# Loading four key units in other pieces, and keeping a row of x on the chip

## The chip, the cores and the metric

The kernel runs on one core of a Trainium2 chip. The metric is the device time of one execution in microseconds (us). Engines are named as in the profile: PE (TensorE), DVE (VectorE), ACT (ScalarE), POOL (GpSimd) and SP (SyncE). SP computes nothing here; it issues nearly all transfers from the chip's memory (HBM), and the core's 16 DMA engines carry them out.

## The reference

One token goes through two blocks, and their outputs are added to x. Block A is attention with cached keys and values: 16 query heads on 8 key/value heads, 65536 keys of 256 numbers a head. Block B is a gated feed-forward layer with a scalar gate r.

```
xn = layernorm(A_x)                                # 1 x 448
q  = xn @ wq                                       # 16 heads of 256
scores = q . k_cache * 256**-0.5                   # two query heads to a key head
o  = softmax(scores) . v_cache
attn = o @ wo                                      # 4096 -> 448
r  = xn @ w_r
ffn = xn + (silu(xn @ w_gate) * (xn @ w_up)) @ w_down * sigmoid(r)
out = x + attn + ffn
```

K and V are 268 MB each in bf16; everything else together is 12 MB. x is used twice: normalized at the start, and in the last sum.

## The kernel before

**Tiling.** Each of the 8 heads' 65536 keys is cut into 4 units. A unit is 128 keys on each of 128 partitions, 64 KB a partition and 8 MB in all. There are 32 units of K (K0 to K31) and 32 of V. They pass through a ring of three slots of one unit each: the even K units use slot 0, the odd ones slot 1, and the V units slot 2. At the start slot 2 also holds wq and small rows such as x; at the end slots 0 and 1 serve for V as well, and slot 2 for the weights of the last stretch.

**Turns.** The program has 32 turns, one for each K unit. In turn u the unit K_u is scored: 8 sets of 16 columns each, and a half of the unit is 4 sets. For each set PE transposes the keys (written `k_T`, 16 transposes), DVE and ACT copy the result out of PSUM to `kt_all`, and PE multiplies by the queries (`k_QK`). From turn 4 on, after the first four sets, there is a V block: PE weighs the unit V_(u-4) with the softmax numerators of its head (`pe_V`, two runs of 32 matmuls into `ps_o`). So the first four turns have no V work; the scores of head 0 are complete in turn 4, whose first sets still contain the last product of K3, its maximum (`m1p`, `gmax`, `negmax`) and the exponentials (ACT, L590). Only then can the V block of turn 4 run.

**What sets the order.** The order on each engine is written out by hand: the functions append waits (`W`) and operations (`O`) to one list for each engine, and `emit` turns the lists into loops. In PE's loop the even and the odd turns have code of their own for the sets, and share the V block. SP's list is a plain sequence: `item` appends the waits a load needs, then the load, and SP stands still at a wait until it is met, with all later loads behind it. The sequence is wq, K0, K1, K2, K3, V0, K4, K5, V1, K6, V2, K7 and so on. The waits are:

- K_u needs its slot: `FREE` of u-2 says that PE has transposed all 8 sets of K_(u-2), `FREEH` that it has transposed the first 4.
- V_t needs `VFREE` of t-1: PE has finished the V block of V_(t-1). V0 needs the end of the setup, since wq lies in its slot.
- PE in turn u waits for the landing of K_u, in the V block for the landing of V_(u-4). Each wait is on a semaphore that the load raises when it lands.

**Pieces.** `HALVED` lists the K units that are loaded in two halves by two transfers with semaphores of their own (`slot0` or `slot1`, and `half0` or `half1`). PE waits for the first half before set 0 and for the second before set 4 (L774). Of a halved unit the first half's load waits for `FREEH` only. Before the change the units 0 to 4 are halved, and all others come whole.

**Setup and end.** In the setup DVE normalizes x (`dve_setup`), PE turns it into a column (`XNT`), multiplies by wq (`QROW`) and puts q where the turns need it (`QT`). `middle` is the part of the end that handles the feed-forward layer; there x is wanted again, normalized (`XN_AGAIN`, L881) and as it is (`YX`, L890). For that the row x is loaded a second time into slot 2, behind w_down and on its semaphore `wd`. PE adds the resulting sum into `ps_s` (`FIN_BASE`) before it turns to the last two V units. PSUM has eight banks; `ps_m` and `ps_s` are two of them and hold small results of each turn in columns below 288.

Of the kernel before, what the change touches and what calls it, by code (L numbers as in the profile page):

```python
# [7 lines left out]
ALU = mybir.AluOpType  # L8
# [4 lines left out]
CH = 64  # L13
# [11 lines left out]
def bass_parallel_sum__gqa_block_cached__moe_arch_mod__decode_kernel(  # L25
# [41 lines left out]
    NT = U * (Hkv - 1)  # L67
    NU = U * Hkv
    NTB = NG
    UH = U + 1  # L70
    HALVED = (0, 1, 2, 3, 4)
    assert rep == 2 and NH == 2 and U * SBN == NPP and U % 2 == 0
    assert 2 * D % P == 0 and RP % 2 == 1 and FK % 2 == 0 and Hq % 2 == 0 and FB <= 512
    inv_sqrt_dh = float(Dh) ** -0.5
# [8 lines left out]
    FO = rep * NH  # L83
    WOA = (Hkv - 1) * WON
    WEN = WOA + WGN + 2 * WDN
    assert WEN + 2 * D <= SLOT
    DC = D // 4

    sb = []
# [11 lines left out]
    wo_all = slots[2][:, 0:WOA]  # L101
    wg_area = slots[2][:, WOA:WOA + WGN]
    wd_area = slots[2][:, WOA + WGN:WOA + WGN + 2 * WDN]
    x_again = slots[2][0:1, WEN:WEN + D]
    xn_again = slots[2][0:1, WEN + D:WEN + 2 * D]
    wo_end = kt_all[:, 0:WON]
    temp = [WQN]

# [84 lines left out]
    ps_m = PS_("ps_m", [P, 512], FP32)  # L193
    C_XNT, C_BC, C_TOT, C_OT, C_Q, C_BIG = 0, 16, 18, 22, 28, 64
    C_HT = C_Q
    assert C_Q + NH * Hq + 4 <= C_BIG and C_HT + FK <= C_BIG and C_BIG + P <= 512

    sems = {}
# [5 lines left out]
        sems[name] = s.__enter__()  # L204
        return name

    for n_ in ["pe", "act", "dve", "pool", "qk", "jt", "evq", "exp", "pc", "qc", "sc", "w0", "out", "wq", "wg", "wo", "wd", "we0", "we1", "we2", "wo2", "wo3", "half0", "half1", "res"]:
        SEM(n_)
    for i in range(NTB):
        SEM(f"ev{i}")  # L210
# [85 lines left out]
    def k_item(u):  # L296
        need = [("FREE", u - 2)] if u >= 2 else ()
        if u >= 2 and u in HALVED:
            need = {0: [("FREEH", u - 2)], 1: need}
        slot_item("k", u, u % 2, [("slot%d" % (u % 2), CH), ("half%d" % (u % 2), CH)] if u in HALVED else None, need)  # L300

    def v_item(t):
        slot_item("v", t, 2, None, [("VFREE", t - 1)] if t else [("QT",), ("R",), ("CONST",)])

    WQ1 = WQN // 4
    item("wq", [(wq_area[:, a:b], flat_src(A_wq, WQN)[:, a:b], "wq") for a, b in ((0, WQ1), (WQ1, WQN))])
    for u in range(U):
        k_item(u)
    v_item(0)
# [61 lines left out]
    def dve_setup():  # L371
        v = nc.vector
        W("dve", "z_m1p")
        O("dve", "XEZ", lambda it: v.memset(xe_row[:, :, :, :], 0.0), "sc")
        O("dve", "PSQ_ZERO", lambda it: v.memset(ps_q[:, :], 0.0), "ev0")
        O("dve", "PSO_ZERO", lambda it: v.memset(ps_o[:, :], 0.0), "ev1")
        O("dve", "s2z0", lambda it: v.memset(s2[0][:, :], 0.0), "ev2")
        O("dve", "pssz", lambda it: v.memset(ps_s[:, :], 0.0))
        O("dve", "S2Z", lambda it: v.memset(s2[1][:, :], 0.0))
        W("dve", "DMA", "w0")  # L380
        O("dve", "xf", lambda it: v.tensor_copy(out=x_f, in_=x_row))
        W("dve", "xf")
        O("dve", "mean", lambda it: v.tensor_reduce(out=stat[0:1, 0:1], in_=x_f, axis=AX.X, op=ALU.add))
        W("dve", "mean")
        O("dve", "negmean", lambda it: v.tensor_scalar(out=stat[0:1, 7:8], in0=stat[0:1, 0:1], scalar1=-1.0 / D, scalar2=None,
                                                       op0=ALU.mult))
        W("dve", "negmean")
        O("dve", "xc", lambda it: v.tensor_scalar(out=xc_f, in0=x_f, scalar1=stat[0:1, 7:8], scalar2=None, op0=ALU.add))
        W("dve", "xc")
        O("dve", "sumsq", lambda it: v.tensor_tensor_reduce(out=xn_f, in0=xc_f, in1=xc_f, scale=1.0, scalar=0.0,  # L390
                                                            op0=ALU.mult, op1=ALU.add, accum_out=stat[0:1, 1:2]))
        W("dve", "sumsq")
        O("dve", "VPE", lambda it: v.tensor_scalar(out=stat[0:1, 2:3], in0=stat[0:1, 1:2], scalar1=1.0 / D, scalar2=EPS,
                                                   op0=ALU.mult, op1=ALU.add))
# [13 lines left out]
        alias("dve", "XE")
        O("dve", "R", lambda it: v.tensor_tensor_reduce(out=x_f, in0=xn_bf, in1=wr_row, scale=1.0, scalar=0.0,
                                                        op0=ALU.mult, op1=ALU.add, accum_out=stat[0:1, 5:6]))  # L410
# [32 lines left out]
    def pe_setup():  # L443
        W("pe", "XE")
        W("pe", "CONST")

        def xnt(it):
            for c in range(2 * NE):
                ins = mm(ps_m[0:P, C_XNT + c:C_XNT + c + 1],
                         lhsT=xe_row[0:1, :, :, :].rearrange("o b c p -> o (b c) p")[:, c, :],  # L450
                         rhs=sel_bf[0:1, 0, 0:1], start=True, stop=True)
            return ins

        O("pe", "XNT", xnt, n=16 * U)
        W("pe", "XNTSB")
        W_item("pe", "wq")

        def qrow(it):
            for h in range(RP):
                for j in range(NG):  # L460
                    ins = mm(q_rows[32 * j:32 * j + rep, :], lhsT=xnT_sb[:, 2 * h:2 * h + 2], rhs=wq_area[:, (NG * h + j) * QN:(NG * h + j + 1) * QN],
                             start=h == 0, stop=h == RP - 1, tile_position=(0, 32 * j))
            return ins

        W("pe", "PSQ_ZERO")
        O("pe", "QROW", qrow, "jt", 2)
        W("pe", "QROWSB")

        def qt(it):
            half = Hq * NH // 2  # L470
            for f in range(half // NG):
                w = q_row[0:QROWS, f // NH * Dh:(f // NH + 1) * Dh].rearrange("s (x f) -> s x f", f=NH)[:, :, f % NH]
                ins = mm(ps_m[0:P, C_Q:C_Q + 2 * half].rearrange("p (i j f) -> p j i f", i=rep, j=NG)[:, :, :, f], lhsT=w,
                         rhs=sel_bf[0:QROWS, :, :], start=True, stop=True)
            return ins

        O("pe", "QT", qt, "qk", 2)
        W("pe", "PSO_ZERO")
        W("pe", "S2Z")
        W("pe", "KZ")  # L480
        W("pe", "z_q")
# [191 lines left out]
    def pe_attn():  # L673
# [9 lines left out]
        oT_i = oT_b.rearrange("p f h i -> p f (h i)")  # L683
        at = [C_BIG + sum(NH * h * h for _, h, _ in WPIECES[:k]) for k in range(len(WPIECES) + 1)]
        sums = picked[:, at[-1] - C_BIG:at[-1] - C_BIG + FO * (Hkv - 1)]
        assert at[-1] <= 512 and at[-1] - C_BIG + FO * (Hkv - 1) <= 256

        def regroup(it):
            for k, (_, h, h0) in enumerate(WPIECES):
# [80 lines left out]
    def k_sets(u, sets, at):  # L770
        ap = slots[u % 2]
        for q in sets:
            if q % CSETS == 0:
                W_item("pe", ("k", u, 0) if q == 0 else ("k", min(u, UH - 1 - (UH - 1 - u) % 2), 1))  # L774
            s = u * SETS + q
            for n, m in enumerate(TORD):
                k_T(s, m, ap, q * SETN)
                if n == NG - 1 and (q + 1) % CSETS == 0:
                    alias("pe", "FREE" if q == SETS - 1 else "FREEH", u, sem=f"t{m}")
                if (q, n) in at:  # L780
                    at[(q, n)]()
                if n == 1:
                    k_QK(s - 1)
            k_JT(s - 2)
# [89 lines left out]
    def middle(T):  # L874
# [2 lines left out]
        pe_ffn1()  # L877
        pe_ffn_hT()
        pe_ffn2()
        W_item("dve", "wd")  # L880
        O("dve", "XN_AGAIN", lambda it: nc.vector.tensor_scalar(out=xn_again, in0=x_again, scalar1=stat[0:1, 7:8], scalar2=stat[0:1, 4:5],  # L881
                                                                op0=ALU.add, op1=ALU.mult))
        W("dve", "XN_AGAIN")
        W("dve", "FFN2")
        W("dve", "ATTN")
        W("dve", "SIG")
        O("dve", "YS", lambda it: nc.vector.scalar_tensor_tensor(
            out=sum_f, in0=ps_y, scalar=stat[0:1, 6:7], in1=xn_again, op0=ALU.mult, op1=ALU.add))
        W("dve", "YS")
        O("dve", "YX", lambda it: nc.vector.tensor_tensor(out=sum_f, in0=sum_f, in1=x_again, op=ALU.add))  # L890
        W("dve", "YX")
        O("dve", "SUM", lambda it: nc.vector.tensor_tensor(out=sum_f, in0=ps_a, in1=sum_f, op=ALU.add))
        W("pe", "SUM")
        W("pe", "SCOPY", T)
# [324 lines left out]
```

## Time and profile before

| | |
|---|---|
| Median of 3 runs | 1275.97 us (1275.46 to 1275.99) |
| Profiled execution | 1275.56 us, span 1274.2 us |
| PE, DVE, ACT busy | 74%, 45%, 26% |
| Transfers | 549.03 MB, queue busy 99.7%, 431 GB/s |
| Granted PE clock, mean | 0.887 of full speed |

The span is the time from the first to the last instruction in the trace of one profiled execution; the 1.36 us by which that execution is longer lie outside of it. Busy shares are means over the whole span; PE's is not an amount of useful work, since its matmuls overlap. The transfers' line counts the time in which packets were on the way, as a share of the span of the 16 DMA engines.

### The profile page before, as it was taken

The page shows a single profiled execution, that of the slowest core. Times are in us where ns is not written, and L with a number is a line of the kernel's source. Part 1 is how long each engine was busy: PE and PEld are TensorE (multiplying, and loading weights), DVE is VectorE, ACT ScalarE, POOL GpSimd, SP SyncE. Part 2 cuts the span into 40 slices and gives each one's busy share as a digit, 9 for nine tenths or more (in the row PEclk, how much of TensorE's full clock was granted, in tenths as well). Part 3 has the DMA queues.
Part 4 walks back from the last instruction along what each step waited for, and adds up shares of the span by engine and source line. Part 5 has one row for each costly group of instructions (what it writes and reads, how often), then busy time and mean ns, then how long its engine had stood idle before and what let it go on. Part 6 is the DMA issues. An engine that isn't in the chain of part 4 may idle for free.

```text
span 1274.2 us, 21262 instructions
## 1 busy us (share of the span) xinstructions
PE 939.5 (74%) x8812; PEld 577.8 (45%) x8812; DVE 571.6 (45%) x1086; ACT 329.3 (26%) x432; POOL 9.1 (1%) x38
## 2 busy tenths in 40 slices
PE   4997977678777679777778776687676687766744
PEld 2665544445444445444445444454344454444412
DVE  5775644355344454443454444454444543434410
ACT  1333422132222322222222222222222222222200
POOL 2000000000000000000000000000000000000000
PEclk9998988789888898888898888898888988888885
DMA  9999999999999999999999999999999999999998
GB/s 405 429 435 426 451 430 430 432 432 434 442 430 430 432 432 436 440 430 430 432 432 440 436 432 428 432 432 440 436 432 428 434 430 446 432 430 428 431 437 364
DMA packets 11812, 549.18 MB, mean 431 GB/s; under 512 B 1303, under 2 KB 1690, under 8 KB 2202
## 3 DMA queue, kind: packets, MB, share of 16 engines
q1 hardware_dynamic: 11796, 549.03, 99.7%
q8 instruction: 7, 0.11, 0.0%
q14 instruction: 3, 0.02, 0.0%
q10 hardware_dynamic: 6, 0.00, 0.0%
HBM read 549.03 MB, written 0.00 MB: 431 GB/s over the span
## 4 chain that ended last, share of the span: by engine, by line
DMA 78%; PE 20%; issue 1%; DVE 0%; ACT 0%; SPq 0%; DVEq 0%
DMA ring<-in_A_v_cache_dram 74%; PE ps_o L441 13%; DMA ring<-in_A_k_cache_dram 5%; PE ps_t L441 5%; PE ps_q L441 1%; PE ps_m L441 1%; PE ps_s L441 0%; DVE kt_all L504 0%; ACT S_sb L590 0%; SPq L983 0%; DVE m1p L560 0%; DVE S_sb L558 0%; ACT p_sb L600 0%; DVE kt_all L932 0%; DVE diag L575 0%
## 5 line engine op out<-in xcount | busy, mean ns | idle before, releaser
L441 PE MATMUL ps_t<-ident_f,ring 128*128 128x128 f32 x4096 | 583.8, 288 | 76.8 <-DMA ring<-in_A_k_cache_dram 76.4
L504 DVE COPY kt_all<-ps_t 128x1024 bf16<-128x1024 bf16 x768 | 489.8, 684 | 293.2 <-PE ps_q L441 287.5
L441 PEld LDWEIGHTS ps_t<-ident_f,ring 128*128 128x128 f32 x4096 | 454.2, 144 | 251.5 <-issue 133.8
L506 ACT ACTIVATE kt_all<-ps_t 128x1024 bf16<-128x1024 bf16 x256 | 261.9, 1023 | 490.1 <-PE ps_t L441 489.8
L441 PE MATMUL ps_o<-ring,p_sb 128*4 128x512 bf16 x2048 | 183.1, 522 | 217.8 <-DMA ring<-in_A_v_cache_dram 214.7
L441 PEld LDWEIGHTS ps_o<-ring,p_sb 128*4 128x4 bf16 x2048 | 54.7, 103 | 313.5 <-issue 292.3
L441 PE MATMUL ps_q<-kt_all,q_pad 128*16 128x512 bf16 x2056 | 168.0, 402 | 4.7 <-DVE kt_all L504 1.3
L613 DVE RECIPROCAL rs<-ps_m 128x4 f32<-128x4 f32 x29 | 5.3, 183 | 277.3 <-PE ps_m L441 277.3
L600 ACT ACTIVATE p_sb<-S_sb 128x128 bf16<-128x128 bf16 x64 | 18.9, 307 | 274.7 <-PE ps_o L441 274.4
L648 DVE CAST ob_sb<-ps_o 100x512 bf16<-100x512 f32 x29 | 20.1, 692 | 101.3 <-PE ps_o L441 101.3
L441 PEld LDWEIGHTS ps_q<-kt_all,q_pad 128*16 128x16 bf16 x2056 | 28.8, 86 | 51.7 <-issue 26.7
L532 ACT ACTIVATE s<-ps_q 112x512 bf16<-112x512 f32 x33 | 19.7, 597 | 118.3 <-PE ps_q L441 118.3
L441 PEld LDWEIGHTS ps_m<-rowsum,ones_f 128*128 128x128 f32 x58 | 12.3, 264 | 23.1 <-issue 23.1
L590 ACT ACTIVATE S_sb<-S_sb,negmax 128x512 bf16<-128x512 bf16 x16 | 13.3, 856 | 23.3 <-DVE negmax L584 23.3
L441 PE MATMUL ps_m<-diag,ones_f 2*128 2x2 f32 x58 | 11.1, 258 | 11.2 <-DVE diag L575 11.2
L441 PEld LDWEIGHTS ps_m<-diag,ones_f 2*128 2x128 f32 x58 | 8.6, 184 | 18.1 <-DVE diag L575 18.1
L560 DVE TENSOR_REDUCE m1p<-S_sb (+1 forms) x33 | 13.9, 422 | 4.4
L441 PE MATMUL ps_m<-rowsum,ones_f 128*128 128x4 f32 x58 | 14.9, 326 | 0.0
L558 DVE CAST S_sb<-ps_s 128x256 f32 (+1 forms) x33 | 13.7, 414 | 1.9 <-PE ps_s L441 1.9
L441 PE MATMUL ps_m<-sel_bf,ring 1*128 1x1 bf16 (+1 forms) x12 | 0.6, 168 | 13.6 <-DVE ring L406 12.8
L441 PE MATMUL ps_s<-sel_bf,s 128*128 128x64 bf16 x132 | 9.2, 193 | 0.7 <-ACT s L532 0.7
L532 ACT ACT_TABLE_LOAD x7 | 9.0, 1283 | 1.3 <-issue 1.2
(97 smaller groups left out, 132.4 us busy)
## 6 DMA issues: line engine op xcount, KB each, us to landing
ring<-in_A_k_cache_dram SPq DMA_DIRECT2D x10, 4096.0 KB, 28.6
ring<-in_A_v_cache_dram SPq DMA_DIRECT2D x2, 4096.0 KB, 27.9
ring<-in_A_wq_dram SPq DMA_DIRECT2D x1, 2688.0 KB, 11.1
ring<-in_B_w_gate_dram SPq DMA_DIRECT2D x1, 1568.0 KB, 16.4
ring<-in_B_w_up_dram SPq DMA_DIRECT2D x1, 1568.0 KB, 19.8
ring<-in_B_w_down_dram SPq DMA_DIRECT2D x1, 1568.0 KB
ring<-in_A_wo_dram SPq DMA_DIRECT2D x1, 1344.0 KB, 35.2
ring<-in_A_wo_dram SPq DMA_DIRECT2D x1, 1120.0 KB, 24.9
```

Source lines behind the costliest of these rows:

```text
L441: return pe.matmul(*a, **k)
L504: O(e, ("EV", s, m), lambda it: nc.vector.tensor_copy(out=kt[:, :], in_=tb[:, :]), f"ev{m}")
L506: O(e, ("EV", s, m), lambda it: nc.scalar.activation(out=kt[:, :], in_=tb[:, :], func=ACTF.Copy), f"ev{m}")
L532: O("act", ("EVQ", u), lambda it: nc.scalar.activation(out=s2[u % 2][0:SROWS, :], in_=ps_q[0:SROWS, :], func=ACTF.Copy), "evq")
L558: O("dve", ("SCOPY", u), lambda it: nc.vector.tensor_copy(out=S_sb[:, at(it, SBN), :], in_=ps_sn), "sc")
L560: O("dve", ("SMAX", u), lambda it: nc.vector.tensor_reduce(out=m1p[:, :, at(it, 1)], in_=S_sb[:, at(it, SBN), :].rearrange("p n i -> p i n ...
L590: O("act", ("EXP", h, i), lambda it, i=i: nc.scalar.activation(out=S_sb[:, :, i], in_=S_sb[:, :, i], func=ACTF.Exp, bias=negmax[:, i:i + 1 ...
L600: O("act", ("PC", t, c), lambda it: nc.scalar.activation(out=p_sb[:, c, :, :], in_=S_sb[:, n:n + CH, :], func=ACTF.Copy), "pc")
L613: O("dve", ("RS", t), lambda it: nc.vector.reciprocal(out=rs[:, :, :], in_=ps_m[0:P, C_TOT:C_TOT + NH * rep]))
L648: O("dve", ("OB", t), lambda it: nc.vector.tensor_copy(out=ob_sb[0:OROWS, :], in_=ps_o[0:OROWS, :]))
```

## The change

Three things are changed.

1. `HALVED` holds only unit 3. The units 1, 2 and 4 are loaded whole, on one semaphore each. Unit 0 comes in three parts of 32, 32 and 64 columns (`FIRST`) on the semaphores `slot0`, `part` and `half0`. PE waits for them before sets 0, 2 and 4. Since even turns share their code, each even turn has these two further waits with constant values, which unit 0's landing has met for good.
2. The two loads of wq have semaphores of their own, `half1` and `wq`. The first stands in for the second half of unit 1 (`items[("k", 1, 1)]`), so that the values for which the odd turns wait in front of set 4 keep their steps.
3. x is not loaded again. In the setup DVE copies the row in two halves of 224 numbers, as fp32, to the last columns of `ps_m` and `ps_s` (`XKEEP`), and at the end `XN_AGAIN` and `YX` read it there, in two pieces each.

```diff
-    HALVED = (0, 1, 2, 3, 4)
+    HALVED = (3,)
+    FIRST = (CH // 2, CH // 2, CH)
...
+    C_X = 512 - D // 2
+    X_HALVES = [(ps_m[0:1, C_X:512], 0, D // 2), (ps_s[0:1, C_X:512], D // 2, D)]
...
-        slot_item("k", u, u % 2, [("slot%d" % (u % 2), CH), ("half%d" % (u % 2), CH)] if u in HALVED else None, need)
+        parts = [("slot%d" % (u % 2), CH), ("half%d" % (u % 2), CH)] if u in HALVED else None
+        slot_item("k", u, u % 2, parts if u else list(zip(("slot0", "part", "half0"), FIRST)), need)
...
-    item("wq", [(wq_area[:, a:b], flat_src(A_wq, WQN)[:, a:b], "wq") for a, b in ((0, WQ1), (WQ1, WQN))])
+    for k, (a, b, sem) in enumerate(((0, WQ1, "half1"), (WQ1, WQN, "wq"))):
+        item(("wq", k), [(wq_area[:, a:b], flat_src(A_wq, WQN)[:, a:b], sem)])
+    items[("k", 1, 1)] = items[("wq", 0)]
...
-    item("wd", [(wd_area.rearrange("p (s x) -> p s x", s=2), B_w_down.rearrange("(s p t) n -> p s (t n)", s=2, p=P), "wd"), (x_again, A_x[0], "wd")])
+    item("wd", [(wd_area.rearrange("p (s x) -> p s x", s=2), B_w_down.rearrange("(s p t) n -> p s (t n)", s=2, p=P), "wd")])
...
+        W("dve", "pssz")
+        for k, (kept, a, b) in enumerate(X_HALVES):
+            O("dve", ("XKEEP", k), lambda it, kept=kept, a=a, b=b: v.tensor_copy(out=kept, in_=x_row[:, a:b]))
         W("dve", "SQRT")
...
-            if q % CSETS == 0:
-                W_item("pe", ("k", u, 0) if q == 0 else ("k", min(u, UH - 1 - (UH - 1 - u) % 2), 1))
+            if q == 0:
+                W_item("pe", ("k", u, 0))
+            elif u % 2 == 0 and q * SETN in (FIRST[0], FIRST[0] + FIRST[1]):
+                W_item("pe", ("k", 0, 1 if q * SETN == FIRST[0] else 2))
+            elif u % 2 and q == CSETS:
+                W_item("pe", ("k", min(u, HALVED[-1]), 1))
...
-        W_item("dve", "wd")
-        O("dve", "XN_AGAIN", lambda it: nc.vector.tensor_scalar(out=xn_again, in0=x_again, scalar1=stat[0:1, 7:8], scalar2=stat[0:1, 4:5],
+        for k, (kept, a, b) in enumerate(X_HALVES):
+            W("dve", "XKEEP", k)
+            O("dve", ("XN_AGAIN", k), lambda it, kept=kept, a=a, b=b: nc.vector.tensor_scalar(
+                out=xn_again[:, a:b], in0=kept, scalar1=stat[0:1, 7:8], scalar2=stat[0:1, 4:5], op0=ALU.add, op1=ALU.mult))
```

SP's first loads before the change, with the semaphores that stand ahead of them (128x16384 is a half of a unit, 128x32768 a whole one; `sem_t2` carries `FREE` and `FREEH`, `sem_pe` carries `VFREE`):

```order
L983 DMA ring<-in_A_wq_dram 128x3584
L983 DMA ring<-in_A_wq_dram 128x10752
L983 DMA ring<-in_A_k_cache_dram 128x16384 x4
L983 DMA ring<-in_A_k_cache_dram 128x16384 [waits sem_t2] x4
L983 DMA ring<-in_A_v_cache_dram 128x32768 [waits sem_pool,sem_dve,sem_qk]
L983 DMA ring<-in_A_k_cache_dram 128x16384 [waits sem_t2] x2
L983 DMA ring<-in_A_k_cache_dram 128x32768 [waits sem_t2]
L983 DMA ring<-in_A_v_cache_dram 128x32768 [waits sem_pe]
```

The same place after it:

```order
L1001 DMA ring<-in_A_wq_dram 128x3584
L1001 DMA ring<-in_A_wq_dram 128x10752
L1001 DMA ring<-in_A_k_cache_dram 128x8192 x2
L1001 DMA ring<-in_A_k_cache_dram 128x16384
L1001 DMA ring<-in_A_k_cache_dram 128x32768
L1001 DMA ring<-in_A_k_cache_dram 128x32768 [waits sem_t2]
L1001 DMA ring<-in_A_k_cache_dram 128x16384 [waits sem_t2] x2
L1001 DMA ring<-in_A_v_cache_dram 128x32768 [waits sem_pool,sem_dve,sem_qk]
L1001 DMA ring<-in_A_k_cache_dram 128x32768 [waits sem_t2] x2
L1001 DMA ring<-in_A_v_cache_dram 128x32768 [waits sem_pe]
```

The order of the units is the same. Unit 0 is three loads, the units 1, 2 and 4 one each, and the load of V1 (the last row of both) still follows K5.

PE's code of the even turns around the V block, before the change (`ps_o` is the V block, the `ps_t` row behind it is the first transpose of set 4):

```order
L441 MATMUL ps_o<-ring,p_sb 4x512 [waits sem_slot2,sem_dve,sem_pc]
L441 MATMUL ps_o<-ring,p_sb 4x512 x31
L441 MATMUL ps_m<-rowsum,ones_f 128x4 [waits sem_pc,sem_dve]
L441 MATMUL ps_o<-ring,p_sb 4x512 [waits sem_slot2,sem_pc]
L441 MATMUL ps_o<-ring,p_sb 4x512 x31
L1108 UNCONDITIONAL_BRANCH
L1142 COMPARE_AND_BRANCH
L1086 REGISTER_ALU
L441 MATMUL ps_t<-ident_f,ring 128x128 [waits sem_ev0,sem_half0]
```

And after it:

```order
L449 MATMUL ps_o<-ring,p_sb 4x512 [waits sem_slot2,sem_dve,sem_pc]
L449 MATMUL ps_o<-ring,p_sb 4x512 x31
L449 MATMUL ps_m<-rowsum,ones_f 128x4 [waits sem_pc,sem_dve]
L449 MATMUL ps_o<-ring,p_sb 4x512 [waits sem_slot2,sem_pc]
L449 MATMUL ps_o<-ring,p_sb 4x512 x31
L1126 UNCONDITIONAL_BRANCH
L1160 COMPARE_AND_BRANCH
L449 MATMUL ps_t<-ident_f,ring 128x128 [waits sem_ev0,sem_half0]
```

The V block stands where it stood, behind four sets of its turn. The wait for `half0` in front of set 4 is now for a constant, so the register operation ahead of it is gone.

DVE's last steps on x at the end, before the change:

```order
L761 CAST hT_sb<-ps_m 128x7x2 [waits sem_pe]
L881 TENSOR_SCALAR ring<-ring,stat 1x448 [waits sem_wd]
L887 SCALAR_TENSOR_TENSOR ring<-ps_t,stat,ring 1x448 [waits sem_ev3,sem_pe,sem_dve]
L890 TENSOR_TENSOR ring<-ring 1x448 [waits sem_dve]
L892 TENSOR_TENSOR ring<-ps_q,ring 1x448 [waits sem_dve]
```

And after it:

```order
L770 CAST hT_sb<-ps_m 128x7x2 [waits sem_pe]
L895 TENSOR_SCALAR ring<-ps_m,stat 1x224
L895 TENSOR_SCALAR ring<-ps_s,stat 1x224
L902 SCALAR_TENSOR_TENSOR ring<-ps_t,stat,ring 1x448 [waits sem_pe,sem_ev3,sem_dve]
L906 TENSOR_TENSOR ring<-ring,ps_m 1x224 [waits sem_dve]
L906 TENSOR_TENSOR ring<-ring,ps_s 1x224
L910 TENSOR_TENSOR ring<-ps_q,ring 1x448 [waits sem_dve]
```

Two of the five steps are cut in two, and the wait for `wd` is gone from DVE.

## Rows read from the trace of the kernel before

**Rows 1.** The page: span, transfer queue, bytes, chain by engine.

```profile
span 1274.2 us, 21262 instructions
...
q1 hardware_dynamic: 11796, 549.03, 99.7%
...
HBM read 549.03 MB, written 0.00 MB: 431 GB/s over the span
...
DMA 78%; PE 20%; issue 1%; DVE 0%; ACT 0%; SPq 0%; DVEq 0%
```

**Rows 2.** Chain of waits, 79 to 250: start us, us, what.

```profile
79.63 40.50 DMA ring<-in_A_k_cache_dram
...
140.15 28.39 DMA ring<-in_A_v_cache_dram
...
174.92 32.32 DMA ring<-in_A_v_cache_dram
...
213.15 32.79 DMA ring<-in_A_v_cache_dram
```

**Rows 3.** Single issues on L983 (K2's first half, V0, K5): start, landing.

```profile
L983 SPq DMA_DIRECT2D ring<-in_A_k_cache_dram x1: 328/328/328, 35.0 to 35.0; - x1
...
DMA to landing us min/median/max: 26.9/26.9/26.9
...
L983 SPq DMA_DIRECT2D ring<-in_A_v_cache_dram x1: 349/349/349, 68.9 to 68.9; - x1
...
DMA to landing us min/median/max: 41.5/41.5/41.5
...
L983 SPq DMA_DIRECT2D ring<-in_A_k_cache_dram x1: 327/327/327, 112.3 to 112.3; - x1
...
DMA to landing us min/median/max: 36.9/36.9/36.9
```

**Rows 4.** Timeline, turns 0 to 2: start us, us, what [idle before <-releaser].

```profile
11.76 0.38 DVE L400 CAST ring<-ring 1x448 bf16<-1x448 f32 x1
...
22.08 1.97 PE L441 MATMUL ps_t<-ident_f,ring 128*128 128x128 f32 x8 [4.13 <-DMA ring<-in_A_k_cache_dram]
...
46.35 0.33 SPq L983 DMA_DIRECT2D ring<-in_A_k_cache_dram  x1
...
68.46 0.33 SPq L983 DMA_DIRECT2D ring<-in_A_k_cache_dram  x1
```

**Rows 5.** Timeline of turn 4, up to V0's last matmuls.

```profile
120.17 1.97 PE L441 MATMUL ps_t<-ident_f,ring 128*128 128x128 f32 x8 [7.89 <-DMA ring<-in_A_k_cache_dram]
...
133.78 0.15 DVE L584 TENSOR_SCALAR negmax<-ps_m 128x2 f32<-128x2 f32 x1
...
136.06 1.90 PE L441 MATMUL ps_o<-ring,p_sb 128*4 128x512 bf16 x32 [1.99 <-ACT p_sb L600]
...
138.21 1.90 PE L441 MATMUL ps_o<-ring,p_sb 128*4 128x512 bf16 x32
```

**Rows 6.** Timeline of turn 5: its first transposes and negmax.

```profile
149.69 2.25 PE L441 MATMUL ps_t<-ident_f,ring 128*128 128x128 f32 x16
...
162.44 0.15 DVE L584 TENSOR_SCALAR negmax<-ps_m 128x2 f32<-128x2 f32 x1
```

**Rows 7.** First load's issue, size and landing; windows (PEclk, DMA share, GB/s last).

```profile
0.81 0.39 SPq L983 DMA_DIRECT2D ring<-in_A_wq_dram  x1
...
ring<-in_A_wq_dram SPq DMA_DIRECT2D x1, 896.0 KB, 5.1
...
0.80:1.80 1.00, 0.00 (x0) 0.00 (x0) 0.21 (x1) 0.20 (x1) 0.91 (x7) 1.00 0.03 1
...
115.00:125.00 10.00, 4.83 (x25) 3.65 (x26) 1.29 (x2) 1.89 (x4) 0.00 (x0) 0.51 0.99 424
```

**Rows 8.** Timeline of the end: the sum with x, and PE's wait behind it.

```profile
1221.90 0.61 DVE L890 TENSOR_TENSOR ring<-ring 1x448 f32<-1x448 f32 x1
...
1227.62 5.48 PE L441 MATMUL ps_o<-ring,p_sb 128*4 128x512 bf16 x64 [4.05 <-DMA ring<-in_A_v_cache_dram]
```

More of the change, by code (lines that the diff above doesn't have):

```diff
@@ L69, in bass_parallel_sum__gqa_block_cached__moe_arch_mod__decode_kernel @@
     NTB = NG
-    UH = U + 1
-    HALVED = (0, 1, 2, 3, 4)
+    HALVED = (3,)
+    FIRST = (CH // 2, CH // 2, CH)
     assert rep == 2 and NH == 2 and U * SBN == NPP and U % 2 == 0
@@ L85, in bass_parallel_sum__gqa_block_cached__moe_arch_mod__decode_kernel @@
     WEN = WOA + WGN + 2 * WDN
-    assert WEN + 2 * D <= SLOT
+    assert WEN + D <= SLOT
     DC = D // 4
@@ L103, in bass_parallel_sum__gqa_block_cached__moe_arch_mod__decode_kernel @@
     wd_area = slots[2][:, WOA + WGN:WOA + WGN + 2 * WDN]
-    x_again = slots[2][0:1, WEN:WEN + D]
-    xn_again = slots[2][0:1, WEN + D:WEN + 2 * D]
+    xn_again = slots[2][0:1, WEN:WEN + D]
     wo_end = kt_all[:, 0:WON]
@@ L195, in bass_parallel_sum__gqa_block_cached__moe_arch_mod__decode_kernel @@
     C_HT = C_Q
+    C_X = 512 - D // 2
+    X_HALVES = [(ps_m[0:1, C_X:512], 0, D // 2), (ps_s[0:1, C_X:512], D // 2, D)]
+    assert C_BIG + P <= C_X and SBN * rep <= C_X
     assert C_Q + NH * Hq + 4 <= C_BIG and C_HT + FK <= C_BIG and C_BIG + P <= 512
@@ L205, in SEM @@
         return name
-    for n_ in ["pe", "act", "dve", "pool", "qk", "jt", "evq", "exp", "pc", "qc", "sc", "w0", "out", "wq", "wg", "wo", "wd", "we0", "we1", "we2", "wo2", "wo3", "half0", "half1", "res"]:
+    for n_ in ["pe", "act", "dve", "pool", "qk", "jt", "evq", "exp", "pc", "qc", "sc", "w0", "out", "wq", "wg", "wo", "wd", "we0", "we1", "we2", "wo2", "wo3", "half0", "half1", "part", "res"]:
         SEM(n_)
@@ L455, in pe_setup @@
         W("pe", "XNTSB")
-        W_item("pe", "wq")
+        W_item("pe", ("wq", 0))
+        W_item("pe", ("wq", 1))
         def qrow(it):
@@ L685, in pe_attn @@
         sums = picked[:, at[-1] - C_BIG:at[-1] - C_BIG + FO * (Hkv - 1)]
-        assert at[-1] <= 512 and at[-1] - C_BIG + FO * (Hkv - 1) <= 256
+        assert at[-1] <= C_X and at[-1] - C_BIG + FO * (Hkv - 1) <= 256
         def regroup(it):
@@ L879, in middle @@
         pe_ffn2()
-        W_item("dve", "wd")
-        O("dve", "XN_AGAIN", lambda it: nc.vector.tensor_scalar(out=xn_again, in0=x_again, scalar1=stat[0:1, 7:8], scalar2=stat[0:1, 4:5],
-                                                                op0=ALU.add, op1=ALU.mult))
-        W("dve", "XN_AGAIN")
+        for k, (kept, a, b) in enumerate(X_HALVES):
+            W("dve", "XKEEP", k)
+            O("dve", ("XN_AGAIN", k), lambda it, kept=kept, a=a, b=b: nc.vector.tensor_scalar(
+                out=xn_again[:, a:b], in0=kept, scalar1=stat[0:1, 7:8], scalar2=stat[0:1, 4:5], op0=ALU.add, op1=ALU.mult))
+        for k in range(len(X_HALVES)):
+            W("dve", "XN_AGAIN", k)
         W("dve", "FFN2")
@@ L889, in middle @@
         W("dve", "YS")
-        O("dve", "YX", lambda it: nc.vector.tensor_tensor(out=sum_f, in0=sum_f, in1=x_again, op=ALU.add))
-        W("dve", "YX")
+        for k, (kept, a, b) in enumerate(X_HALVES):
+            O("dve", ("YX", k), lambda it, kept=kept, a=a, b=b: nc.vector.tensor_tensor(
+                out=sum_f[:, a:b], in0=sum_f[:, a:b], in1=kept, op=ALU.add))
+        for k in range(len(X_HALVES)):
+            W("dve", "YX", k)
         O("dve", "SUM", lambda it: nc.vector.tensor_tensor(out=sum_f, in0=ps_a, in1=sum_f, op=ALU.add))
```

## The prediction, made before the result was known

> **What bounds the kernel now.** I read the page first: its transfer queue is occupied for 99.7% of the span and moves 549.03 MB at 431 GB/s, and 78% of the chain that ended last is DMA [rows 1]. So the end is set by one stream of loads that never stops. A change can move the end only by shortening this stream, by leaving a hole in it, or by lengthening the last stretch behind it.
>
> Second, the chain of waits, for the pace of the stream. A transfer's landing is its issue plus its piece in the chain: V1 lands at 140.15 + 28.39 = 168.54, V2 at 174.92 + 32.32 = 207.24, V3 at 213.15 + 32.79 = 245.94 [rows 2]. Two landings are 38.70 us apart with one K unit and one V unit between them, so a whole unit takes 19.35 us and each lands exactly that long behind the one before it. The queue is full as long as SP issues the next load before the last one queued has landed. That margin is what I look for: V2 is issued at 174.92, and K6 ahead of it lands at 168.54 + 19.35 = 187.89, a margin of 13.0 us. For V1 it is smaller: K5 lands at 112.3 + 36.9 = 149.2 [rows 3], V1 is issued at 140.15 [rows 2], a margin of 9.0 us. It is the smallest one behind the first V unit, and the change is made there.
>
> Third, the timeline of turn 4, for what V1's issue hangs on. V1 needs V0's slot, which comes free when PE has done the V block of turn 4. That block stands behind the first four sets of K4. PE starts them at 120.17 after 7.89 us of waiting for K4, DVE writes negmax at 133.78, the V block runs from 136.06 to 140.11 (138.21 + 1.90) [rows 5]. K4's first half lands at 79.63 + 40.50 = 120.13 [rows 2], so V1 is issued 20.02 us after the landing that starts turn 4.
>
> **The change part by part.**
>
> *Fewer, larger loads of K.* Unit 2's first half lands at 35.0 + 26.9 = 61.9 and V0 at 68.9 + 41.5 = 110.4 [rows 3]; three halves and a whole unit lie between. (48.5 - 19.35) / 3 = 9.72 us a half, so a unit in two halves takes 0.08 us more than one in a piece. Units 1, 2 and 4 lose a split each, unit 0 gains one: two transfers fewer up to K4, -0.16 us.
>
> The Trainium skill ("DMA: Bandwidth & Descriptors", Anatomy of one DMA) puts a fixed 2.0 us on each DMA beside its bytes, fitted on the gpsimd path. Three DMAs fewer would be worth -6 us by it. The rows above disagree: in a queue that is full a further transfer costs 0.08 us.
>
> *Unit 0 in three parts, and the setup.* Half of unit 0 takes 9.7 us, and PE waits for the first one until 22.08 [rows 4], so the first quarter lands near 22.1 - 4.9 = 17.2. PE is through with the setup at 22.08 - 4.13 = 17.95 [rows 4]. DVE gains two casts of 1x224 ahead of the reciprocal; a cast of 1x448 takes 0.38 [rows 4], so about 0.4 us in all, bounds 0 (behind the wait for ACT's square root) and 0.8 (two whole casts). PE then starts at about 18.3 instead of 22.08, does two sets, finds the second quarter there, and waits for the second half, which lands at 61.9 - 3 x 9.72 = 32.7. Four sets take 11.3 us (35.0 to 46.35, [rows 3, 4]): unit 0 is read by 44.0 instead of 46.35. Nobody waits for that: the stream still has K1 until 52.2 (61.9 - 9.7). Gain 0.
>
> *Units 1 and 2 whole.* PE now waits for all of K1, from 44.0 to 52.2, and starts it where it used to start its first half at 46.35: 5.8 us later. Its two halves take 12.9 (22.08 to 35.0, a start from rest) and 11.3 us, a later unit 22.1 (46.35 to 68.46) [rows 3, 4]. Against the stream: K2 is issued at 44.0, K1 lands at 52.2, margin 8; K3's first half needs half of unit 1, 65.1, K2 lands at 71.5, margin 6; K3's second half needs all of it, 76.4, and the half before it lands at 81.2, margin 5; K4 needs unit 2, 98.5, V0 lands at 110.2, margin 12; K5 needs unit 3, 120.6, K4 lands at 129.7, margin 9. PE stands later everywhere, but the queue stays full: 0 us. The bounds are 0 and, if PE lost 5 us more, a hole at K3's second half.
>
> *Unit 4 whole.* This is the term. Turn 4 now waits for all of K4. That lands one unit before K5: 149.2 - 19.35 = 129.85, less 0.16, so 129.7, where the half landed at 120.13. What follows in turn 4 is the same work in the same order on PE, so V1 is issued 20.02 us later, at 149.7. K5 lands at 149.05. **The last transfer in the queue has landed 0.65 us before the next one is issued**, so the stream runs dry, and the issue of V1 waits on PE with everything behind it on SP's queue.
>
> How long the hole is depends on how a transfer starts in an empty queue, and the trace has one such start, the first. It is issued at 0.81 and the window from 0.8 to 1.8 moves nothing to speak of (1 GB/s): at least 1.0 us goes before bytes flow [rows 7]. The first 896 KB land 5.1 us after their issue [rows 7], and at 431 GB/s they are 2.1 us of work: 3.0 us of overhead at most. I take 2.6, nearer to the upper row, since that one is a whole load by the same queue into the same tile; the ramp of a first start may not all come back. V1 then lands at 149.7 + 19.35 + 2.6 = 171.65 instead of 168.54: +3.1 us, with bounds of +1.5 and +3.5 from the overhead. The 20.02 us is uncertain too. PE starts turn 4 from rest, at a granted clock of 0.51 between 115 and 125 (mostly the 1.2 GHz level) [rows 7], and takes 13.61 us to negmax [rows 5]; turn 5, started while running, takes 162.44 - 149.69 = 12.75 [rows 6]. In the changed kernel PE rests about as long before turn 4 (9.1 us for 7.89), so I expect the slow form; the warm one would give 0.9 us back, a longer slow stretch cost some 0.5.
>
> The Trainium skill gives a first-byte latency of about 0.6 us for a DMA from the sync queue (the same page, Latency and other measured facts). With it alone for the overhead the hole would be 1.1 us. The first start, with 1.0 us empty and 3.0 in all, does not bear it out.
>
> Behind V1 the stream stays late for good. K6 needs only the last four sets of K4, 11.3 us after V1's issue, with V1 itself 22 us in flight; from there on the margins are those of now.
>
> *x kept in PSUM.* The 0.9 KB load between w_down and wo goes: up to 0.08 us, by the price above. At the end DVE does x's normalization and its last sum in two pieces of 224 instead of one of 448. The sum took 0.61 us [rows 8]; two pieces cost at most 0.6 us more. PE idles 4.05 us behind them for V30 [rows 8], so 0.
>
> **Sum.** -0.16 is already in K4's time; +3.1 for the hole, about -0.05 for x: +3.05. The profiled execution took 1275.56, a span of 1274.2 and 1.36 around it, and is 0.41 below the median of the runs. On the median: 1275.97 + 3.05 = 1279.0; I say **1279.1 us**. About 0.2%, 2.55 us, is what a measurement of this kernel can tell from no change, and the forecast lies just above it.
>
> **Rivals.** (a) *The hole is there but short*, +0.5 to +2.5 us: the queue restarts after 1.0 us and no more, or turn 4 runs warm. For it: nothing shows a second start of the queue, and PE is capable of 12.75 us. Against it: the one start seen. Price at 1.0 us of overhead: +1.5, 1277.5 us.
>
> (b) *No hole, not slower.* PE would have to free V0 early enough for V1's first bytes to reach the queue by K5's landing: 19.35 - 1.0 = 18.35 us after K4's landing instead of 20.02. From that point on the rest is the saved splits, -0.2, 1275.8 us. Even the warm form with 19.2 us misses it by 0.8 us.
>
> (c) *A second hole*, at K3's second half (margin 5) or K5 (margin 9), if PE loses that much more in turns 1 to 3, for instance by a low clock after its 8 us of rest. Another 2 to 3 us: 1282. Against it: the 12.9 us that I used contains such a start from rest.
>
> (d) *Every DMA costs its fixed price in the stream*, as a mechanism of this kernel: three fewer, and less to do on SP. By the skill's 2.0 us that would be 1270 us; the rows allow 0.08 each.
>
> **How the numbers follow.** Hole of +2.6 to +3.8 us: 0.64. (a) 0.22, (b) 0.06, (c) 0.05, (d) 0.03. Faster holds (d), 0.03; slower holds the forecast, (c), and a little of the upper end of (a), 0.70; the rest, 0.27, is within 0.2%. The range leaves out (d), (b), part of (c) and the lowest part of (a): 1277.1 to 1280.7; the likeliest case's own range is 1278.5 to 1279.8.
>
> **What would show it.** In the profile after: PE waits for K1 from about 44 to 52; turn 4 starts at 129.7; SP issues V1 at 149 to 150.5, and it lands 21 to 22.4 us later instead of 28.39; a window from 149 to 152 shows the transfer rate falling, and no other window behind the start does; V landings are again 38.70 apart from V1 to the end, all 1.5 to 3.5 us late; the last stretch is as now. I am wrong if V1 is issued before 148, if the rate never falls, or if a second hole stands in the first 100 us.

## The result, and the profile after

| | before | after |
|---|---|---|
| Median (7 runs each) | 1275.77 us (1275.46 to 1275.99) | 1280.04 us (1279.48 to 1281.86) |
| Profiled execution, its span | 1275.56, 1274.2 us | 1279.79, 1278.4 us |

The changed kernel is slower: the ratio is 1.0036 [1.0025, 1.0047], 4.3 us. The forecast, 1279.1, is 0.9 us below the median and the range holds it; the predicted step was +3.05 on 1275.97, the measured one is +4.27, and +4.2 between the two spans.

The page after: span, then the transfer rate in 40 slices of 32 us, the queue, the bytes, the chain by engine.

```profile
span 1278.4 us, 21265 instructions
...
GB/s 409 430 437 433 377 427 437 445 431 427 427 451 435 427 427 435 445 433 427 427 445 441 427 427 427 449 437 427 427 429 451 433 427 427 443 439 431 417 446 356
...
q1 hardware_dynamic: 11506, 549.03, 99.4%
...
HBM read 549.03 MB, written 0.00 MB: 429 GB/s over the span
...
DMA 78%; PE 20%; DVE 1%; issue 1%; SPq 0%; ACT 0%; DVEq 0%
```

The bytes are the same, the rate over the span is 429 GB/s instead of 431 [rows 1], and one slice stands out: the fifth, 128 to 160 us, with 377. That is where the hole was forecast.

Turn 4 in the timeline after (start us, us, what, idle before it and who ended it), which answers to [rows 5]:

```profile
129.69 1.97 PE L449 MATMUL ps_t<-ident_f,ring 128*128 128x128 f32 x8 [10.29 <-DMA ring<-in_A_k_cache_dram]
...
143.17 0.15 DVE L593 TENSOR_SCALAR negmax<-ps_m 128x2 f32<-128x2 f32 x1
...
145.45 1.90 PE L449 MATMUL ps_o<-ring,p_sb 128*4 128x512 bf16 x32 [1.99 <-ACT p_sb L609]
...
147.60 1.90 PE L449 MATMUL ps_o<-ring,p_sb 128*4 128x512 bf16 x32
...
149.54 0.33 SPq L1001 DMA_DIRECT2D ring<-in_A_v_cache_dram  x1
```

PE starts at 129.69 instead of 120.17, with K4's landing, and V1 is issued behind the V block's end (147.60 + 1.90 = 149.50), 9.4 us later than before. Whether the queue is empty by then is read from the issues of K5 and V1 after (start, then issue to landing):

```profile
L1001 SPq DMA_DIRECT2D ring<-in_A_k_cache_dram x1: 328/328/328, 119.4 to 119.4; - x1
...
DMA to landing us min/median/max: 29.6/29.6/29.6
...
L1001 SPq DMA_DIRECT2D ring<-in_A_v_cache_dram x1: 328/328/328, 149.5 to 149.5; - x1
...
DMA to landing us min/median/max: 21.9/21.9/21.9
```

K5 lands at 119.4 + 29.6 = 149.0, half a microsecond before V1's issue at 149.54, and V1 lands at 171.4 instead of 168.54. The windows across it (busy us of PE, PEld, DVE, ACT and POOL with counts, then the granted clock, the DMA share and GB/s; a packet is credited to the window in which it starts, so that the zeros count here, while a short window can overshoot):

```profile
145.00:148.00 3.00, 2.55 (x42) 1.17 (x46) 0.18 (x1) 1.79 (x6) 0.00 (x0) 1.00 0.25 109
148.00:149.00 1.00, 1.00 (x24) 0.47 (x20) 0.00 (x0) 0.00 (x0) 0.00 (x0) 1.00 0.00 0
149.00:150.00 1.00, 1.00 (x17) 0.58 (x6) 0.45 (x1) 0.31 (x1) 0.00 (x0) 1.00 0.00 0
150.00:151.00 1.00, 1.00 (x13) 0.39 (x11) 0.24 (x1) 0.00 (x0) 0.00 (x0) 1.00 2.83 983
```

Behind it the chain is as regular as in [rows 2]:

```profile
176.29 33.82 DMA ring<-in_A_v_cache_dram
...
216.94 31.88 DMA ring<-in_A_v_cache_dram
```

V2 and V3 land at 210.11 and 248.82, 38.7 us apart and each 2.9 us later than before. So 2.9 of the 4.2 us are the hole. The rest comes at the end, between two of the last weight loads. First before, then after, the issues of w_up and of wo (w_down stands between them in the queue):

```profile
L983 SPq DMA_DIRECT2D ring<-in_B_w_up_dram x1: 433/433/433, 1181.9 to 1181.9; - x1
...
DMA to landing us min/median/max: 19.8/19.8/19.8
...
L983 SPq DMA_DIRECT2D ring<-in_A_wo_dram x1: 340/340/340, 1183.2 to 1183.2; - x1
...
DMA to landing us min/median/max: 24.9/24.9/24.9
```

```profile
L1001 SPq DMA_DIRECT2D ring<-in_B_w_up_dram x1: 433/433/433, 1184.2 to 1184.2; - x1
...
DMA to landing us min/median/max: 20.4/20.4/20.4
...
L1001 SPq DMA_DIRECT2D ring<-in_A_wo_dram x1: 467/467/467, 1185.1 to 1185.1; - x1
...
DMA to landing us min/median/max: 27.2/27.2/27.2
```

w_up lands at 1201.7 before and 1204.6 after: still +2.9. wo lands at 1208.1 and 1212.3: +4.2, and that stays to the end (1274.2 and 1278.4, both 66.1 us later). The step from w_up to wo, by the unrounded landings, is 6.46 us before and 7.73 after: **+1.27 us that the prediction did not have**. In this stretch the transfers by queue (packets, MB, share) show one packet that is no load, before (1202 to 1206) and after (1204.7 to 1209.6):

```profile
q1 hardware_dynamic: 244, 2.13, 126.6%
q8 instruction: 1, 0.02, 1.7%
```

```profile
q1 hardware_dynamic: 302, 2.08, 101.9%
q8 instruction: 1, 0.02, 1.4%
```

It is 16 KB of instructions, and takes 1.08 us in both traces. It runs on one of the 16 DMA engines that carry the loads: while it lasts, 15.2 load packets are on the way on average, and 16.2 right before and behind it (ends and starts overlap a little), in these two and in every kernel below. The first packet behind it takes 0.43 to 0.48 us longer than others of its size. Both kernels have this fetch; only after does it cost anything. What differs is how far the 16 engines are apart. Each of them ends its part of a load with a packet of 4 bytes, and the table has the time from the first engine's last packet of a load to the last engine's (us, from the packets of both traces):

```
                K5     V1     w_up   wo
before          2.07   2.07   2.12   2.14
after           1.93   0.80   0.86   2.13  (15 engines within 0.87, the last 1.26 behind)
```

A load has landed when its last engine is done. Before, the engines are 2.1 us apart from 50 us on; after, the hole lets them start V1 nearly together, they stay 0.8 to 0.9 us apart for a thousand microseconds, and then one of them falls behind all others. The last packets of all 16 engines (us behind the first) show what the fetch does in either trace:

```
before  w_up  0 .04 .22 .26 .28 .28 .33 .34 .36 .61 .75 1.08 1.73 1.80 1.95 2.12
        wo    0 .05 .21 .26 .28 .28 .35 .40 .60 .75 1.07 1.75 1.83 1.89 1.96 2.14
after   w_up  0 .14 .16 .16 .16 .20 .23 .24 .30 .41 .45 .54 .56 .74 .78 .86
        wo    0 .13 .15 .16 .16 .20 .25 .25 .31 .40 .46 .54 .74 .78 .87 2.13
```

Between the two loads one engine loses some 1.55 us in both, the fetch and the longer packet together: before from about 0.34 to 1.89, after from 0.56 to 2.13. Before, four engines already lie 1.7 to 2.1 us behind, and the fifth still ends ahead of the last of them; after, it is the last by 1.26 us, which is the missing term.

### The profile page after: what moved, and what is told of

The parts are those of the page before. It is cut to its first block, busy times and chain, and to the rows that moved or that the text cites. A ratio compares the mean times of both kernels' runs of the same rounds, so it can differ in the third digit from the quotient of the medians.

```text
span 1278.4 us, 21265 instructions
## 1 busy us (share of the span) xinstructions
PE 935.2 (73%) x8812; PEld 572.6 (45%) x8812; DVE 575.0 (45%) x1090; ACT 329.0 (26%) x432; POOL 9.1 (1%) x38
## 4 chain that ended last, share of the span: by engine, by line
DMA 78%; PE 20%; DVE 1%; issue 1%; SPq 0%; ACT 0%; DVEq 0%
DMA ring<-in_A_v_cache_dram 69%; PE ps_o L449 12%; DMA ring<-in_A_k_cache_dram 6%; PE ps_t L449 5%; DMA kt_all<-in_A_wo_dram 3%; PE ps_q L449 1%; PE ps_m L449 1%; SPq L1001 0%; DVE kt_all L513 0%; ACT S_sb L599 0%; DVE m1p L569 0%; PE ps_s L449 0%; DVE S_sb L567 0%; DVE diag L584 0%; DVE gmax L581 0%
## 5 line engine op out<-in xcount | busy, mean ns | idle before, releaser
L449 PEld LDWEIGHTS ps_t<-ident_f,ring 128*128 128x128 f32 x4096 | 449.5, 143 | 266.9 <-issue 135.8
L449 PE MATMUL ps_o<-ring,p_sb 128*4 128x512 bf16 x2048 | 178.4, 511 | 210.5 <-DMA ring<-in_A_v_cache_dram 207.4
## 6 DMA issues: line engine op xcount, KB each, us to landing
ring<-in_A_wq_dram SPq DMA_DIRECT2D x1, 2688.0 KB, 11.1
```

What stands on the lines that cost most here:

```text
L449: return pe.matmul(*a, **k)
```

## The experiments

Two claims were to be tested: that unit 4 in one piece is the whole cause, by V1's lateness and nothing else; and that the last 1.27 us are the fetch on engines that run nearly in step.

**1. Unit 4 (and unit 2) in halves again**, everything else as changed: does the loss hang on it, or on unit 0's parts, unit 1, or x?

```
-    HALVED = (3,)
+    HALVED = (2, 3, 4)
-            elif u % 2 == 0 and q * SETN in (FIRST[0], FIRST[0] + FIRST[1]):
-                W_item("pe", ("k", 0, 1 if q * SETN == FIRST[0] else 2))
+            elif u % 2 == 0 and q * SETN == FIRST[0]:
+                W_item("pe", ("k", 0, 1))
+            elif u % 2 == 0 and q == CSETS:
+                W_item("pe", ("k", min(u, 4), 1) if u else ("k", 0, 2))
-                W_item("pe", ("k", min(u, HALVED[-1]), 1))
+                W_item("pe", ("k", min(u, 3), 1))
```

> The changed kernel with K2 and K4 in halves again; unit 0 still in three parts, K1 whole, x kept in PSUM. Theory A (the hole in front of V1, opened by the whole K4, costs 2.9 us, and 1.3 us more follow from it when an instruction fetch delays one of 16 DMA engines that run nearly in step): turn 4 starts 9.7 us earlier, V1 is issued about 9 us before K5 lands, no window behind the start at 0 GB/s, 1275.7 us (1275.3 to 1276.2). Rival B (the three parts of unit 0, or the copies of x, cost the time): 1279 to 1280 us as in the changed kernel.

1275.69 us, ratio 1.0002 [0.9993, 1.0011]. V1's piece of the chain is issued at 139.53, and the window in which nothing moved is full:

```profile
139.53 28.93 DMA ring<-in_A_v_cache_dram
```

```profile
148.00:150.00 2.00, 2.00 (x22) 1.29 (x20) 1.20 (x4) 0.33 (x2) 0.00 (x0) 1.00 1.14 492
```

w_up to wo is 6.46 again. The other parts of the change (unit 0, unit 1, x) cost nothing together, within -0.9 to +1.4 us.

**2. Unit 4 whole, alone**, in the kernel before.

```
-    UH = U + 1
-    HALVED = (0, 1, 2, 3, 4)
+    UH = U
+    HALVED = (0, 1, 2, 3)
```

> The kernel before with one thing changed: K4 comes whole. x is loaded again, units 0 to 3 in halves. Theory A: V1 issued at about 150, landing near 171.5, all later landings 2.9 us late; from w_up's landing to wo's 7.6 us instead of 6.5, since the engines are in step here too; 1279 to 1280.3 us. Rival C (the second 1.3 us come from the missing load of x): 6.5 us from w_up to wo, 1278.7 us. Rival B: 1275.8 us.

1280.13 us, ratio 1.0037 [1.0024, 1.0051]: all of the loss, with the row of x still loaded between w_down and wo. V1, w_up and wo (issues as above):

```profile
L983 SPq DMA_DIRECT2D ring<-in_A_v_cache_dram x1: 328/328/328, 149.1 to 149.1; - x1
...
DMA to landing us min/median/max: 22.1/22.1/22.1
...
L983 SPq DMA_DIRECT2D ring<-in_B_w_up_dram x1: 432/432/432, 1183.9 to 1183.9; - x1
...
DMA to landing us min/median/max: 20.5/20.5/20.5
...
L983 SPq DMA_DIRECT2D ring<-in_A_wo_dram x1: 344/344/344, 1185.3 to 1185.3; - x1
...
DMA to landing us min/median/max: 27.0/27.0/27.0
```

V1 lands at 171.2, w_up at 1204.5, wo at 1212.3: a step of 7.8. So the late 1.3 us belong to the whole unit 4 as well, and not to the missing load of x.

**3. x kept, alone**, in the kernel before (the core of the edit; `XN_AGAIN` and the waits go the same way).

```
-    item("wd", [(wd_area..., "wd"), (x_again, A_x[0], "wd")])
+    item("wd", [(wd_area..., "wd")])
+        for k, (kept, a, b) in enumerate(X_HALVES):
+            O("dve", ("XKEEP", k), lambda it, ...: v.tensor_copy(out=kept, in_=x_row[:, a:b]))
-        O("dve", "YX", lambda it: nc.vector.tensor_tensor(out=sum_f, in0=sum_f, in1=x_again, op=ALU.add))
+        for k, (kept, a, b) in enumerate(X_HALVES):
+            O("dve", ("YX", k), lambda it, ...: nc.vector.tensor_tensor(
+                out=sum_f[:, a:b], in0=sum_f[:, a:b], in1=kept, op=ALU.add))
```

> The kernel before with x kept in PSUM and not loaded again, K0 to K4 in halves. Theory A: no hole, 6.5 us from w_up to wo, 1275.8 us (1275.4 to 1276.1). Rival C: 7.6 to 7.8 us from w_up to wo, 1277 us. Rival B with the copies of x as the cost: later still.

1275.54 us, ratio 1.0000 [0.9991, 1.0009], w_up to wo 6.48. Nothing is gained or lost by x, to within 1.1 us.

**4. V1 still later**: in the changed kernel its load also waits until PE has read all of K4.

```
-        slot_item("v", t, 2, None, [("VFREE", t - 1)] if t else [("QT",), ("R",), ("CONST",)])
+        need = [("VFREE", t - 1)] if t else [("QT",), ("R",), ("CONST",)]
+        slot_item("v", t, 2, None, need + [("FREE", U)] if t == 1 else need)
```

> The changed kernel with one wait more: V1 is issued only when PE has also transposed all of K4, 10.7 us after the end of the V block. The hole is made longer by a known amount. Theory A (the hole costs, microsecond for microsecond, what the issue of V1 is late, plus about 2.5 us to restart an empty queue): V1 issued at 160.2, landing 21.9 us later at 182.1, every later landing 10.7 us later than in the changed kernel, 1290.7 us (1290 to 1291.7). If the stream could win back lost time, or the restart of a queue that has rested longer costs more or less: a landing clearly off 21.9 us behind the issue, or an end clearly off 1290.7.

1291.08 us, ratio 1.0122 [1.0104, 1.014]. V1 in the chain:

```profile
160.55 21.80 DMA ring<-in_A_v_cache_dram
```

V1 is issued 11.0 us later than in the changed kernel, and the median is 11.0 us higher (the span 11.1): lateness is paid one to one. A unit is 19.35 us of stream, so the restart costs 21.80 - 19.35 = 2.45 here.

**5. V1 in two halves**: the slot's first half comes free when the first half of the V block is done, so half of V1 can be issued before the queue is empty. The half gets the semaphore `half1`; for that PE's wait for it, in the odd turns, moves from set 4 to set 3.

```
-        slot_item("v", t, 2, None, [("VFREE", t - 1)] if t else [("QT",), ("R",), ("CONST",)])
+        need = [("VFREE", t - 1)] if t else [("QT",), ("R",), ("CONST",)]
+        if t == 1:
+            need = {0: [("PVC", 0, 0)], 1: need}
+            slot_item("v", t, 2, [("half1", CH), ("slot2", CH)], need)
...
+            return
+        slot_item("v", t, 2, None, need)
```

> The changed kernel with V1 loaded in two halves: the first waits only for the first run of matmuls of turn 4's V block, about 2.1 us before the whole block is done. K4 stays whole. Theory A: the first half is issued near 147.4, its first bytes are there at about 148.5 to 149, where the slowest DMA engine ends K5, so the hole nearly closes: V1 lands at 168.5 to 169.5, and the end is at 1275.8 to 1278 us, the upper part if the engines, which the short hole still brings into step, meet the instruction fetch again (over 7 us from w_up to wo). If the whole K4 cost its time in another way than by V1's late issue: 1280 us.

1278.74 us, ratio 1.0027 [1.0015, 1.0038]: a part comes back, less than expected (1275.8 to 1278). The two issues of V1, and the windows:

```profile
L1009 SPq DMA_DIRECT2D ring<-in_A_v_cache_dram x1: 328/328/328, 147.1 to 147.1; - x1
...
DMA to landing us min/median/max: 12.8/12.8/12.8
...
L1009 SPq DMA_DIRECT2D ring<-in_A_v_cache_dram x1: 328/328/328, 149.3 to 149.3; - x1
...
DMA to landing us min/median/max: 20.4/20.4/20.4
```

```profile
146.00:148.00 2.00, 2.00 (x38) 0.91 (x34) 0.18 (x1) 0.54 (x2) 0.00 (x0) 1.00 0.15 66
148.00:149.00 1.00, 1.00 (x24) 0.34 (x16) 0.00 (x0) 0.00 (x0) 0.00 (x0) 1.00 1.62 492
```

The issue at 147.12 is 1.9 us ahead of K5's landing at 148.98, and yet the rate falls to 66 GB/s. The first engine is done with K5 at 147.0, and V1's first packet starts at 148.08: engines that are done first run dry before K5 lands. The half takes 12.8 us from issue to landing, where 1.9 of K5's remainder and 9.7 of stream make 11.6, so about 1.2 us are lost. By lateness paid one to one the issue would have to come some 3.1 us (12.8 - 9.7) ahead of the landing to lose nothing; that is an estimate, since no run has a margin between 1.9 and 5 us. V1 is complete at 169.7, 1.2 us later than with a full queue. The engines are then 1.32 us apart, and w_up to wo takes 7.1, between the two other values. These 1.2 and 0.7 us account for most of the profiled execution, whose span is 2.1 us longer than before; it is the fastest of the seven, and the further 1.0 us up to the median are not explained.

**6. The fetch moved by filler code** (`PAD` from 10 to 100, in the changed kernel).

```
-PAD = 10
+PAD = 100
```

> The changed kernel with 100 instead of 10 small filler matmuls ahead of the last stretch (their results are not used, before or after). That moves PE's later code by some 180 instructions against the places where PE's code is fetched; x stays unloaded. Theory A (the second 1.3 us are an instruction fetch that holds up one DMA engine while all run in step): the fetch comes some us earlier, so the lengthening moves to w_gate's or w_up's landing (5.0 us instead of 3.77), and from w_up to wo it is 6.5 us again; 1280 us (1279.5 to 1281) as in the changed kernel. Rival D (w_down's own load is slower after a hole, whatever PE fetches): w_up to wo stays at 7.7 us.

1280.69 us, ratio 1.0038 [1.0023, 1.0052], w_up to wo 7.86. The fetch was expected some microseconds earlier, with the lengthening at w_gate or w_up and 6.5 us from w_up to wo; that did not come. The filler took 2.64 us of PE instead of 0.39, and the fetch still came behind w_up's landing (1205.64), at 1206.44. So the run does not tell the fetch from a slow w_down.

**7. wo ahead of w_down** in the changed kernel: the fetch theory says that the disturbance stays at its time, with whichever load is then on the way; the rival is that w_down or its place in the memory is slow.

```
-    item("wd", [(wd_area.rearrange("p (s x) -> p s x", s=2), B_w_down.rearrange("(s p t) n -> p s (t n)", s=2, p=P), "wd")])
...
+    item("wd", [(wd_area.rearrange("p (s x) -> p s x", s=2), B_w_down.rearrange("(s p t) n -> p s (t n)", s=2, p=P), "wd")])
```

> The changed kernel with the loads of w_down and of the first part of wo in exchanged order; the hole in front of V1 stays. Both lie behind w_up. Without any disturbance wo takes 2.7 us of the stream and w_down 3.8. Theory A (an instruction fetch of PE, about 1.5 us after w_up's landing, holds up one of 16 DMA engines that run in step): whatever load is on the way then is the longer one, so wo takes 4.0 us and w_down 3.8, the sum is 7.7 as in the changed kernel; 1280 us (1279.5 to 1281). Rival D (w_down's own load is slower after a hole): wo 2.7 us, w_down 5.0.

1280.03 us, ratio 1.0038 [1.0023, 1.0052]. The issues of wo and w_down, and the transfers by queue in 1204.8 to 1208.8:

```profile
L1001 SPq DMA_DIRECT2D ring<-in_A_wo_dram x1: 432/432/432, 1184.8 to 1184.8; - x1
...
DMA to landing us min/median/max: 24.0/24.0/24.0
...
L1001 SPq DMA_DIRECT2D ring<-in_B_w_down_dram x1: 434/434/434, 1185.3 to 1185.3; - x1
...
DMA to landing us min/median/max: 27.3/27.3/27.3
```

```profile
q8 instruction: 1, 0.02, 1.7%
```

w_up lands at 1204.74, wo at 1208.81, w_down at 1212.57. w_down takes 3.76 here; wo, now on the way when the fetch comes at 1206.13, takes 4.07, where 6.46 - 3.76 = 2.70 is its undisturbed time. The 1.3 us stand with the load that meets the fetch, in either order, and a slow w_down is out. That any load right behind w_up would be slow, fetch or not, is out by the packets: here too one of the 16 is missing for just as long as the fetch lasts.

The step from w_up to wo over all kernels (7: to the later of wo and w_down):

```
no hole      before 6.46   (1) 6.46   (3) 6.48
short hole   (5) 7.13
hole         after 7.73    (2) 7.81   (4) 7.92   (6) 7.86   (7) 7.83
```

## Why the prediction was right, and where it fell short

*The bound.* Right: one stream of loads sets the end, and the end moved only by its interruptions.

*Splits, units 0, 1 and 2, x: nothing.* Right, by experiments 1 to 3. PE's waits moved as worked out: it waits for K1 until 52.3, and V1's predecessors in the queue are all issued at least 5 us before the load ahead of them lands. One size was off without consequence. Unit 0's first part lands at 17.3, but PE starts it at 20.85 and not at 18.3:

```profile
20.85 1.62 PE L449 MATMUL ps_t<-ident_f,ring 128*128 128x128 f32 x8 [2.68 <-issue]
```

PE waited for nothing that the trace shows ("issue"); the casts of x are not it, since the reciprocal behind them moved by only 0.25 us. Nobody waits for PE there. At the end the sum with x takes 0.38 and 0.37 us for 0.61, and PE's wait for V30 is still there, 2.57 us for 4.05 [rows 8]:

```profile
1231.82 1.45 PE L449 MATMUL ps_o<-ring,p_sb 128*4 128x512 bf16 x12 [2.57 <-DMA ring<-in_A_v_cache_dram]
```

*Unit 4: the hole.* Right, with its numbers, and shown by experiments 1 and 2 as the whole cause: K4 landed at 129.64 (129.7 forecast), V1 was issued 19.90 us behind that (20.02), K5 landed at 149.0 (149.05), the restart cost 21.89 - 19.35 = 2.54 (2.6), V1 was 2.9 us late (3.1). The 2.6 was a choice between 1.0 and 3.0 from the only start in the trace, so that it came so close is in part luck. PE's slow form was the right choice: negmax came 13.48 us after turn 4's start, against 13.61 in the slow form of [rows 5] and 12.75 in the warm one of [rows 6]. The granted clock over these stretches was 0.85, 0.81 and 1.00: turn 4 starts at the 1.2 GHz level in both kernels, after PE has waited 10.29 and 7.89 us. What the restart consists of can be read from the packets of V1. Its first packet starts 0.96 us after the start of the issue in the changed kernel and in experiments 2, 4 and 5, about as in the kernel's first start (1.0). But the last of the 16 engines starts 1.6 to 2.1 us after it (changed kernel, experiments 4 and 2), and the first packets take 2.5 to 3.3 us, those behind them 2.42. The Trainium skill ("DMA: Bandwidth & Descriptors", Latency and other measured facts) has about 0.6 us to the first byte. The trace agrees if one counts from the end of the issuing instruction (0.63 us), but in none of the three restarts (2.54, 2.74, 2.45 us) was that all.

*Rivals.* (a), a short hole, falls: the restart was not 1.0 us. Experiment 5 shows that (b) was also priced too kindly: V1 issued 1.9 us ahead of K5's landing still lost 1.2, so that PE would have had to free V0 some 3 us ahead by the estimate there, not 1.0. (c) did not come: no other slice or landing shows a second hole. (d) is out by experiment 3, which drops a load and gains nothing, and by K4's landing: with two loads fewer up to it, it came at 129.64 instead of 129.84 (K4's second half before), 0.20 us earlier.

**The step that failed** is "the last stretch is as now", and with it "all 1.5 to 3.5 us late" up to the end: the sum had one term where there are two. The missing one is +1.27 us (4.2 = 2.9 + 1.3). The prediction treated the queue as one server that is late by the hole and otherwise as before. It is 16 engines, and a landing is the last of them. The likeliest case's own range, 1278.5 to 1279.8, does not hold the 1280.04; the stated range does because it leaves room for part of (c), a second hole, which did not come. That is luck.

That the extra time goes with an instruction fetch meeting the load on the way is shown by experiment 7; that it comes only with the hole, by experiments 1 to 3; that the engines are closer together behind a hole, and that the fetch costs nothing before because it falls on an engine 1.8 us ahead of the last, by the packets. Open is which engine takes a fetch: that could not be steered, and no run shows one falling on a late engine in the kernel before. Why PE idles those 2.68 us at the start is open too.

## What to carry to other kernels

In a kernel bound by one stream of loads, look for the smallest margin between the issue of a load and the landing of the one ahead of it: a larger piece starts its reader later, the reader frees the next slot later, and when the margin is gone the stream pays the lateness one to one plus a restart. Count the margin as safe only when it is a restart's length above zero, some 3 us here by the estimate of experiment 5. And a stream over several engines ends with the last of them: where a change has brought the engines into step, small disturbances can count that did not count before.

## What the runs showed of the hardware

- The restart of an empty queue cost 2.45 to 2.74 us beside the bytes (after, experiments 2 and 4), of which 0.96 passed before the first packet; an issue 1.9 us ahead of the last landing still left a gap (experiment 5).
- Instructions are fetched in packets of 16 KB, mostly 1.0 to 1.1 us each, and the fetch takes one of the 16 DMA engines from the loads; with the longer packet behind it the engine falls back by some 1.5 us. Four in the first 50 us of the kernel before (at 24.5, 34.3, 43.0 and 48.6) let the engines grow apart from 0.9 to 2.1 us: of the loads that end at 21.6, 32.0, 41.9 and 51.8, none, one, two and four engines are more than 1.5 us behind. They stay so for 1150 us in a full queue, and a hole brings them back to 0.8.
- A single fetch behind the hole moved the end by 1.3 us, and nothing took it back.
